# Tile 3's gate and value products as three units of seven half-size products, with the order behind tile 1's middle written anew

## The chip, the cores and the metric

The kernel runs on one core of one Trainium2 chip. The metric is the device time of one execution in microseconds (us), the median over several runs.

## The reference

Two parts, one behind the other. First a linear attention with decay, over blocks of 64 positions (q, k and v are 4 batches × 8 heads × 768 positions × 64):

```python
for b in range(nb):
    intra = np.einsum('bhic,bhjc->bhij', qb, kb) * Dmask[None]
    intra = np.einsum('bhij,bhjd->bhid', intra, vb)
    inter = np.einsum('bhid,bhde->bhie', qb * lam_pow[None], kv_state)
    out[:, :, sl] = intra + inter
    kb_dec = kb * rev_pow[None]
    kv_state = lam_block[None, :, None, None] * kv_state + np.einsum('bhsd,bhse->bhde', kb_dec, vb)
```

Then a gated feed-forward network on the attention's output as x (3072 tokens × 512, inner width 1536):

```python
g = x @ w_gate
silu = g * (1.0 / (1.0 + np.exp(-g)))
val = x @ w_val
return (silu * val @ w_out).astype(np.float32)
```

Inputs and output are float32; the kernel multiplies in bfloat16 and sums in float32.

## The kernel before, in words

**Tiles and groups.** The tokens are cut into 6 FFN tiles of 512 (t = 0 to 5), and the attention into 12 groups of 256 tokens (g = 0 to 11); groups 2t and 2t+1 make tile t's input, `xt`. A state per batch runs from group to group, so the groups of one batch must come in order.

**A group's way through the engines.** SyncE (SP in the profile) loads its k, q and v (`load_fp32`, L103). The keys are cast by `kcast` (L277, mostly ScalarE, ACT), the queries scaled by `qcast` (L281, VectorE, DVE, or GpSimd, POOL), both are turned by one transposing DMA (`dma_transpose`, L265, issued by SP), and v is scaled (`v_scale`, L257). On TensorE (PE) follow `scores` (32 small matmuls; the causal `mask` L356 on DVE carries them to SBUF), `upd_mm` (L390, the state's increments), `inter` (L530, the query with the state) and `intra` (L547, the scores with v). Inter and intra sum into the same two banks; between them ACT reads one column of a bank (`guard`, L523), and intra waits for that. `sadd` (L485, DVE) adds the increments to the state step by step, `kvn` (L503) casts each step for inter, `kvm` (L507) and `kv0c` (L511) pass the state on to the next group of the batch. `evr` (L566) evicts the two banks into `xt`, on ACT with few exceptions.

**An FFN tile.** The inner width is 12 chunks of 128. For tiles 0 to 3, `ffn_gate` (L592) and `ffn_val` (L607) each do 4 matmuls a chunk: 512 columns each, or 256 for half a tile; `HALVED` (L585) names chunks of which each matmul is cut in two. ACT takes the SiLU of the gate (L605), DVE multiplies (L622) into `h`.

Tiles 4 and 5 use a scheme with seven products in place of eight for a 2 × 2 block multiplication. `unit` (L721) takes two chunks of each half of the inner width, so that three units make up a tile; `uprod(t, j, k, i)` (L731) is product k (0 to 6) of unit j, for the gate (i = 0) or the value (i = 1): 4 matmuls of 256 columns, so 14 such products make a unit. Behind k = 0 and k = 1 ACT copies a bank (L759 into the bank Bb, L761 into the buffer es), behind k = 2 and k = 4 DVE adds Bb and es (L763 into the bank E, L765 into es). `silu` (L770) and `mu` (L776) make h out of the four quarters; `mup` (L515) is the quarter whose two inputs both lie in SBUF. The products need sums of the weights (`w_combo`, L686: four for the gate, four for the value; the last, n = 3, overwrites the second-half weights in place) and of x (`x_combo`, L707: four a tile, the last in place). Once the weights are overwritten, no plain chunk from 6 on can be done any more.

The output product is of the same kind for tiles 1 to 5: `hsum` (L665, four sums of h, in pieces along the chunks), `oprod` (L799, product k = 1 to 7 of half a tile, 6 matmuls of 256 columns), `store` (L792). Tile 0 uses plain products (`ffn_out`, L629).

**The order.** Nothing is scheduled by a planner at run time: the calls stand in the order in which each engine gets its instructions, some 800 lines from L838 on. `use(...)` names the banks (of PSUM's eight) that the next helper takes; `unit`, `out_new` and `op_new` take theirs for longer. TensorE runs through its own instructions in that order, and so does every other engine; a wait at the head of an engine's queue holds up all that stands behind it. The DMAs of loads, transposes and stores are issued by SP in their order. Some 1,030 lines in, tile 1's chunks are half done; tile 2's chunks, tile 3's chunks, groups 4 to 11, the output products and the units of tiles 4 and 5 follow, interleaved.

Tile 3 before is 12 gate and 12 value chunks of 512 columns. Groups 8, 9 and 10 are attended between its chunks and behind. Group 10's `inter` (L1422) stands in unit (4, 0) and its `intra` (L1437) in unit (4, 1); group 8's is this, L1302 to L1310:

```python
    use(1, 5); op_new(8)
    inter(8, True)
    use(6, 0); scores(9)
    use(4, 3); upd_mm(9)
    sadd(9, 0)
    guard(8)
    kvn(9, 0, ACTC)
    sadd(9, 1)
    intra(8, False)
```

## Time and profile before

| | us |
|---|---|
| median of 3 runs | 215.95 (215.81 to 216.06) |
| profiled execution, its own time | 215.75 |
| its span | 214.04 |
| TensorE busy | 207.5 |
| VectorE busy | 157.5 |
| ScalarE busy | 131.8 |
| GpSimd busy | 50.9 |

The span is the time between the first and the last instruction in the trace; the execution's own time has 1.71 us around it. An engine's busy time is the union of its instructions (register work, semaphores and the issuing of DMAs are not counted). The chain of waits goes back from the last instruction, at each step to what released it. Times of rows are microseconds from the span's start, and a row such as `117.15 2.59 PE bank L618 x12` gives start, length, engine, output, line and the number of instructions. In the table of groups the numbers behind the bar are busy time, mean nanoseconds of one instruction, and the idle time of the engine ahead of them with what ended it.

### The profile page before, as it was taken

Reading aid. Unit: us, or ns where it says so; the run is one execution under the profiler, and the core shown is the slowest. Engines: PE = TensorE matmul, PEld = TensorE weight load, DVE = VectorE, ACT = ScalarE, POOL = GpSimd, SP = SyncE. Lnnn points to the kernel's source line nnn. Section 1 sums busy time; section 2 is a strip of 40 time slices with the busy share of each in tenths; the row PEclk is TensorE's granted clock in tenths of the full one; section 3 lists DMA queues with packets and bytes.
Section 4 is the critical chain, followed back from the end, with each engine's and each line's share of the span. In section 5 each row is a group of like instructions: output and inputs, shape, how many; then the busy total and the mean of one; then the engine's idle time right before and its main releaser. Section 6 shows DMA issues by size and latency. Waiting matters only on the chain.

```text
span 214.0 us, 6802 instructions
## 1 busy us (share of the span) xinstructions
PE 207.5 (97%) x2801; PEld 153.0 (72%) x2801; DVE 157.5 (74%) x302; ACT 131.8 (62%) x283; POOL 50.9 (24%) x72
## 2 busy tenths in 40 slices
PE   7799999999999999999999999999999999999993
PEld 3466455888886558767654545888888888888883
DVE  1673447679774798889779899999887589982851
ACT  6788576657446443667677385946873677536522
POOL 6585755704472010300101030040200000000200
PEclk9999999999999999999999999999999999999999
DMA  6999999999996697989677869776000500005014
GB/s 187 343 352 373 378 365 324 266 256 222 356 335 132 168 280 188 240 204 261 156 189 163 208 144 248 185 69 228 6 3 3 196 0 3 0 0 199 0 54 147
DMA packets 82177, 39.77 MB, mean 186 GB/s; under 512 B 45410, under 2 KB 77794, under 8 KB 82146
## 3 DMA queue, kind: packets, MB, share of 16 engines
q1 hardware_dynamic: 80946, 38.74, 66.7%
q10 hardware_dynamic: 1200, 0.59, 1.0%
q8 instruction: 22, 0.36, 0.7%
q14 instruction: 9, 0.07, 0.1%
HBM read 28.31 MB, written 6.29 MB: 162 GB/s over the span
## 4 chain that ended last, share of the span: by engine, by line
PE 92%; SPq 3%; DMA 2%; POOL 1%; issue 0%; ACT 0%; DVE 0%
PE bank L814 22%; PE bank L600 20%; PE bank L618 20%; PE bank L755 17%; PE bank L638 5%; SPq L109 2%; DMA v<-in_v_dram 2%; PE bank L541 2%; PE bank L554 2%; PE bank L408 1%; PE bank L347 1%; POOL v_s L260 1%; PE bank L383 1%; PE bank L310 0%; ACT kvf L501 0%
## 5 line engine op out<-in xcount | busy, mean ns | idle before, releaser
L622 DVE TENSOR_TENSOR h<-sil,bank 128x256 bf16<-128x256 bf16 (+1 forms) x67 | 35.0, 532 | 21.4 <-PE bank L618 17.2
L618 PE MATMUL bank<-xt,wv_sb 128*128 128x256 bf16 (+1 forms) x276 | 50.2, 314 | 0.0
L600 PE MATMUL bank<-xt,wg_sb 128*128 128x256 bf16 (+1 forms) x276 | 50.1, 315 | 0.0
L605 ACT ACTIVATE sil<-bank 128x256 bf16<-128x256 f32 (+1 forms) x67 | 31.6, 477 | 22.3 <-PE bank L600 15.7
L618 PEld LDWEIGHTS <-wv_sb 128*128 128x128 bf16 x276 | 26.6, 98 | 14.7
L600 PEld LDWEIGHTS <-wg_sb 128*128 128x128 bf16 x276 | 26.1, 98 | 12.9
L260 POOL TENSOR_TENSOR v_s<-v,dec 128x512 bf16<-128x512 f32 (+1 forms) x15 | 18.6, 1254 | 60.9 <-DMA v<-in_v_dram 19.8
L814 PEld LDWEIGHTS <-h 128*128 128x128 bf16 x240 | 23.5, 98 | 3.6
L814 PE MATMUL bank<-wo_sb,h 128*128 128x256 bf16 x180 | 22.3, 273 | 0.0
L814 PEld LDWEIGHTS <-hs 128*128 128x128 bf16 x180 | 17.5, 98 | 3.4 <-DVE hs L673 0.2
L362 DVE TENSOR_TENSOR ssb<-bank,causal 128x512 bf16<-128x512 f32 x24 | 15.5, 684 | 3.6 <-PE bank L347 3.5
L814 PE MATMUL bank<-wt,hs 128*128 128x256 bf16 x120 | 15.6, 272 | 0.0
L755 PEld LDWEIGHTS <-ws 128*128 128x128 bf16 x144 | 14.0, 98 | 1.8
L755 PE MATMUL bank<-xs,ws 128*128 128x256 bf16 x96 | 13.9, 272 | 0.0
L763 DVE TENSOR_TENSOR bank<-bank,es 128x512 f32<-128x512 f32 x12 | 8.3, 697 | 7.2 <-PE bank L755 4.4
L780 DVE TENSOR_TENSOR h<-sil,bank 128x512 bf16<-128x512 bf16 x18 | 11.8, 679 | 1.5 <-ACT sil L774 1.2
L780 POOL TENSOR_TENSOR h<-sil,es 128x512 bf16<-128x512 bf16 x1 | 1.2, 1162 | 46.7 <-DVE es L765 46.7
L774 ACT ACTIVATE sil<-bank 128x512 bf16<-128x512 f32 x18 | 10.2, 593 | 2.1 <-PE bank L755 2.1
L638 PE MATMUL bank<-wo_sb,h 128*128 128x512 bf16 x48 | 10.9, 379 | 0.0
L755 PE MATMUL bank<-xt,wv_sb 128*128 128x256 bf16 x72 | 10.8, 273 | 0.0
L443 ACT CAST kvn<-kvf 64x256 bf16<-64x256 f32 x22 | 8.9, 403 | 3.1 <-DVE kvf L489 2.7
L278 ACT CAST qk<-kraw 128x1024 bf16<-128x1024 f32 x9 | 9.4, 1042 | 1.8 <-DMA kraw<-in_k_dram 1.8
(127 smaller groups left out, 342.9 us busy)
## 6 DMA issues: line engine op xcount, KB each, us to landing
out_dram<-osb SPq DMA_DIRECT2D x22, 256.0 KB, 2.7
v<-in_v_dram SPq DMA_DIRECT2D x18, 256.0 KB, 4.3
woraw<-in_moe_w_out_dram SPq DMA_DIRECT2D x6, 512.0 KB, 9.1
kraw<-in_k_dram SPq DMA_DIRECT2D x24, 128.0 KB, 3.2
qraw<-in_q_dram SPq DMA_DIRECT2D x24, 128.0 KB, 3.8
wraw<-in_moe_w_gate_dram SPq DMA_DIRECT2D x5, 512.0 KB, 6.9
wraw<-in_moe_w_val_dram SPq DMA_DIRECT2D x5, 512.0 KB, 6.7
kraw<-in_k_dram SPq DMA_DIRECT2D x4, 512.0 KB, 6.3
```

The lines of the kernel that those rows point to most:

```text
L260: eng.tensor_tensor(out=st[("vs", g)][:, h0:h1], in0=st[("v", g)][:, h0:h1].rearrange("p h (s d) -> p h s d", s=2), in1=vfac(g, h0, h1), o ...
L278: fn(out=qk_new(g)[:, 0].rearrange("p s (h d) -> p h s d", h=H), in_=st[("kraw", g)].rearrange("p h (s d) -> p h s d", s=2))
L362: nc.vector.tensor_tensor(out=st[("ssb", g)][:, h2, 2 * c:2 * c + 2].rearrange("p a s n -> p a (s n)"), in0=st[("sp", g, c, h2)].rearrange ...
L600: nc.tensor.matmul(gp[:, n0:n1], wg_sb[:, mc, fs], xt[:, g0:g1, mc].rearrange("p g b n -> p g (b n)"), start=(mc == 0 and n0 == 0), stop=( ...
L605: nc.scalar.activation(sil[:, 0:N], gp[:, 0:N], AF.Silu)
L618: nc.tensor.matmul(vp[:, n0:n1], wv_sb[:, mc, fs], xt[:, g0:g1, mc].rearrange("p g b n -> p g (b n)"), start=(mc == 0 and n0 == 0), stop=( ...
L622: nc.vector.tensor_tensor(out=h_sb[:, fc % FH, b0:b1].rearrange("p b n -> p (b n)"), in0=sil[:, 0:N], in1=vp[:, 0:N], op=ALU.mult)
L638: nc.tensor.matmul(ps, st[("h", t, fc // FH)][:, fc % FH, b], wo_sb[:, fc, c0:c1], start=(fc == 0), stop=(fc == FC - 1))
L755: nc.tensor.matmul(o[i][:, fi * 256:fi * 256 + 256], lhs(c, 2 * j + fi), rhs(c), start=(k < 2 and fi == 0 and c == 0), stop=(c == KH - 1), ...
L774: nc.scalar.activation(sil[half, r], unit_src(t, j, half, r)[0], AF.Silu)
L780: eng.tensor_tensor(out=st[("h", t, half)][:, 2 * j:2 * j + 2][:, :, r:B:2], in0=v3(st[("u", t, j)][4][half, r]), in1=v3(unit_src(t, j, ha ...
L814: nc.tensor.matmul(o, lhs(f), rhs(f), start=(k in (1, 7) and f == 0), stop=(f == FH - 1), skip_group_check=True)
```

## The change

What it does:

- Tile 3 is done in three units of 14 products, like tiles 4 and 5, in place of its 24 chunks. Its sums of x take a buffer of the pool that also holds the transposed queries and keys.
- The sums of the weights come earlier, ahead of tile 3, in 8 calls (they were 10). As they overwrite the second-half weights, tile 2's chunks 6 to 11 now come first (6 to 9 in half tiles), then 0 to 5; `HALVED` names chunks 10 and 11.
- Group 10's inter, guard and intra stand in one place among tile 2's output products. Group 8's stand directly behind each other.
- The order of all that follows tile 1's middle is written anew, with other banks.
- Engines: to POOL go `kcast` of groups 7 and 11, `qcast` of 10 and 11 (`qcast` of 7 was there), `v_scale(7)` and the second half of `v_scale(9)`, `kvm(7)`, `kvn(6, 1)`, `kvn(9, 1)`, all three `kvn` of group 11, `mup` of (3, 1), (4, 0) and (5, 1), and four of tile 5's sums of h. From POOL to DVE go `v_scale(11)`, `kvm(3)` and `kvm(5)`. All evictions from group 3 on are on ACT.

The same before and after: 12 each of scores, updates, inter and intra; the output products; the units of tiles 4 and 5.

```diff
-    HALVED = ((2, 4), (2, 5))
+    HALVED = ((2, 10), (2, 11))
...
-    XS0 = 4
+    XS0 = (3, 4)
...
-            pool, tag = (qkt_pool, "qkt") if t == XS0 else (raw_pool, "raw")
+            pool, tag = (qkt_pool, "qkt") if t in XS0 else (raw_pool, "raw")
```

The part of the new order that holds tile 3 (all lines new in this form):

```diff
+    use(4, 5); op_new(7)
+    oprod(1, 1, 2)
+    oprod(1, 1, 3)
+    oprod(1, 1, 4)
+    inter(7, True)
+    use(0, 3); scores(8)
+    guard(7)
+    intra(7, False)
+    use(6, 7); upd_mm(8)
...
+    v_scale(9, nc.gpsimd, 0, 4)
+    v_scale(9, nc.gpsimd, 4, 8)
...
+    unit(3, 0, (7, 5, 4, 3, 2, 1))
+    uprod(3, 0, 0, 0)
+    hsum(2, 0, 0, 4, 0, 2, nc.vector)
+    x_combo(3, 2, None, nc.vector)
...
     dma_transpose(9)
     load_fp32(10, nc.sync, k, "kraw")
     load_fp32(10, nc.sync, q, "qraw")
+    store(1, 0, 0, 0, 512, None)
+    store(1, 1, 1, 0, 512, None)
+    load_fp32(10, nc.sync, v, "v")
+    silu(3, 0, 0, 1)
+    use(5, 6); upd_mm(9)
     inter(8, True)
+    guard(8)
+    intra(8, False)
+    use(0, 2); scores(9)
     sadd(9, 0)
     kvn(9, 0, ACTC)
     sadd(9, 1)
+    kvn(9, 1, POOLC)
+    sadd(9, 2)
+    mu(3, 0, 1, 0)
+    mask(9, 0, 0)
+    mask(9, 0, 1)
+    hsum(2, 0, 4, 6, 0, 2, nc.vector)
+    evr(8, 0, ACTC)
+    kvn(9, 2, ACTC)
+    unit(3, 1, (6, 0, 5, 2, 3, 7))
+    uprod(3, 1, 0, 0)
+    uprod(3, 1, 1, 0)
+    uprod(3, 0, 4, 1)
+    uprod(3, 1, 0, 1)
+    uprod(3, 1, 2, 0)
+    mup(3, 0, nc.vector)
...
+    kcast(10, ACTC)
+    qcast(10, nc.gpsimd)
     dma_transpose(10)
     load_fp32(11, nc.sync, k, "kraw")
     load_fp32(11, nc.sync, q, "qraw")
     load_fp32(11, nc.sync, v, "v")
+    store(1, 1, 0, 0, 512, None)
+    uprod(3, 1, 4, 0)
+    uprod(3, 0, 6, 1)
+    uprod(3, 1, 5, 0)
+    uprod(3, 1, 3, 1)
+    mu(3, 0, 0, 1)
+    mu(3, 1, 0, 0)
+    hsum(2, 1, 0, 4, 0, 2, nc.vector)
+    uprod(3, 1, 6, 0)
+    uprod(3, 1, 4, 1)
...
+    unit(3, 2, (1, 4, 6, 0, 3, 5))
+    uprod(3, 2, 0, 0)
+    uprod(3, 2, 0, 1)
+    uprod(3, 1, 5, 1)
+    uprod(3, 2, 1, 0)
+    mu(3, 1, 1, 0)
+    hsum(2, 1, 4, 6, 0, 2, nc.vector)
+    uprod(3, 2, 1, 1)
+    uprod(3, 2, 2, 0)
+    uprod(3, 2, 2, 1)
+    uprod(3, 1, 6, 1)
+    uprod(3, 2, 3, 0)
+    silu(3, 2, 0, 0)
+    mu(3, 1, 0, 1)
+    uprod(3, 2, 4, 0)
+    uprod(3, 2, 4, 1)
...
+    mup(3, 1, nc.gpsimd)
+    hsum(2, 2, 4, 6, 0, 2, nc.vector)
+    v_scale(10, nc.gpsimd, 0, 4)
+    kvm(7, nc.gpsimd)
+    v_scale(10, nc.gpsimd, 4, 8)
...
     inter(9, True)
+    use(6, 4); upd_mm(10)
+    use(7, 3); scores(10)
+    guard(9)
+    intra(9, False)
+    kcast(11, POOLC)
+    qcast(11, nc.gpsimd)
```

Tile 2's output products with group 10 in them, and the tail's sums on POOL:

```diff
     oprod(2, 1, 6)
+    x_combo(4, 0, None, nc.vector)
+    oprod(2, 0, 6)
+    x_combo(4, 1, None, nc.vector)
+    hsum(2, 3, 4, 6, 0, 2, nc.vector)
     sadd(10, 0)
     kvn(10, 0, ACTC)
...
+    use(4, 0); op_new(10)
+    oprod(2, 1, 3)
+    inter(10, True)
+    guard(10)
+    oprod(2, 0, 3)
+    use(3, 6); upd_mm(11)
+    intra(10, False)
...
+    hsum(5, 3, 0, 2, 0, 2, nc.gpsimd)
+    mup(5, 1, nc.gpsimd)
+    hsum(5, 0, 2, 4, 0, 2, nc.gpsimd)
+    hsum(5, 2, 2, 4, 0, 2, nc.gpsimd)
+    hsum(5, 3, 2, 4, 0, 2, nc.gpsimd)
+    mup(5, 2, nc.gpsimd)
```

834 lines of the change are left out of this document (395 added, 439 removed).

## The prediction

> **What bounds the kernel now.** I read the page's head first, then the chain of waits, then the busy time by stretch, then the groups by form, and last the timelines around the places that the change touches. A number in the sums has its row quoted ahead of it.
>
> ```profile
> span 214.0 us, 6802 instructions
> PE 207.5 (97%) x2801; PEld 153.0 (72%) x2801; DVE 157.5 (74%) x302; ACT 131.8 (62%) x283; POOL 50.9 (24%) x72
> PE   7799999999999999999999999999999999999993
> PE 92%; SPq 3%; DMA 2%; POOL 1%; issue 0%; ACT 0%; DVE 0%
> ```
> TensorE is busy for 97% of the span and holds 92% of the chain that ended last. Next the chain itself (start, length, engine, work):
>
> ```profile
> 97.01 0.38 PE bank L541 x32
> 98.26 0.97 PE bank L600 x4
> 117.15 2.59 PE bank L618 x12
> 167.86 17.47 PE bank L755 x160
> 210.86 0.28 ACT osb L833
> 211.16 0.29 DVE osb L833
> ```
> From the first tenth of the span to 210.86 each piece begins where the last ended: TensorE is gapless, and it alone sets the end. Here are its unit prices: an FFN matmul of 512 columns takes 2.59/12 = 0.216 us, a half-size product's matmul of 256 columns 17.47/160 = 0.109 us, and the first FFN chunk after an attention block 0.97 instead of 4 × 0.216 = 0.86, so 0.10 for the return. The busy time of the stretch that the change rewrites (columns: stretch; length; PE, PEld, DVE, ACT, POOL busy with counts; granted clock; DMA share; GB/s):
>
> ```profile
> 47.80:110.45 62.65, 62.65 (x975) 45.29 (x976) 50.35 (x93) 35.87 (x79) 14.77 (x13) 1.00 0.94 231
> 110.45:134.47 24.02, 24.02 (x345) 12.23 (x343) 21.58 (x37) 16.29 (x36) 3.10 (x3) 1.00 0.77 189
> 134.47:167.86 33.39, 33.39 (x466) 28.81 (x465) 29.70 (x59) 21.68 (x50) 3.79 (x4) 1.00 0.34 74
> 167.86:210.86 43.00, 42.97 (x393) 38.08 (x390) 29.51 (x59) 24.57 (x52) 1.16 (x1) 1.00 0.16 62
> ```
> The rewritten part starts at 47.80. PE is busy 163.03 of 163.06 us there, at full clock; DVE is next, with 21.58 of 24.02 in the stretch that holds tile 3. So a saving on TensorE is worth its full size as long as the others keep up, and DVE has the least room to.
>
> **The change, part by part.** The prices of what is added on the other engines:
>
> ```profile
> L605 ACT ACTIVATE sil<-bank 128x512 bf16<-128x512 f32 x29 | 17.1, 596 | 11.9 <-PE bank L600 10.5 <-issue 1.2
> L780 DVE TENSOR_TENSOR h<-sil,bank 128x512 bf16<-128x512 bf16 x18 | 11.8, 679 | 1.5 <-ACT sil L774 1.2 <-PE bank L755 0.3
> L763 DVE TENSOR_TENSOR bank<-bank,es 128x512 f32<-128x512 f32 x12 | 8.3, 697 | 7.2 <-PE bank L755 4.4 <-ACT es L761 2.5
> L765 DVE TENSOR_TENSOR es<-bank,es 128x512 f32<-128x512 f32 x12 | 8.2, 685 | 1.0 <-PE bank L755 0.8
> L761 ACT COPY es<-bank 128x512 f32<-128x512 f32 x12 | 6.9, 592 | 1.3 <-PE bank L755 1.2
> L759 ACT COPY bank<-bank 128x512 f32<-128x512 f32 x12 | 6.7, 578 | 0.6 <-ACT sil L774 0.2
> L719 DVE TENSOR_TENSOR xs<-xt,xs 128x512 bf16<-128x512 bf16 x4 | 1.7, 419 | 0.1
> L780 POOL TENSOR_TENSOR h<-sil,es 128x512 bf16<-128x512 bf16 x1 | 1.2, 1162 | 46.7 <-DVE es L765 46.7
> L282 POOL TENSOR_TENSOR qk<-qraw,qdn 128x1024 bf16<-128x1024 f32 x1 | 1.9, 1903 | 11.2 <-DMA qraw<-in_q_dram 11.2
> ```
> *TensorE.* Removed: 24 chunks × 4 matmuls × 0.216 = 20.74. Added: 3 units × 14 products × 4 matmuls × 0.109 = 18.35. That is **−2.4 us**. The other matmuls keep their counts and sizes, and both orders go back from attention to other products 22 times, so these 0.10s cancel. Tile 2's reordered chunks, with other chunks halved, cost nothing: the same number of columns.
>
> *ACT.* Tile 3's 12 activations stay (L605's become L774's). Added are 3 units × 4 copies: 6 × 0.592 + 6 × 0.578 = 7.0; the evictions that DVE did come over and some casts go to POOL. ACT had 98.4 us busy of 163 (the four stretches); with 5 more it is still far from full. Cost nothing as a load; its queue order counts below.
>
> *DVE.* The 12 multiplications stay (0.68 each). Added: 3 × 4 sums, 6 × 0.697 + 6 × 0.685 = 8.3, and four combinations of x, 4 × 0.42 = 1.7. Taken off: two query scalings at 1.22 as POOL gets them, two multiplications, half a value scaling and one whole, a state scaling, four short tail sums, two evictions; put on: the last group's value scaling and two state scalings. Net some 2 us on 131. What the total hides is the place: between the last attention visit of group 7 (106) and the middle of tile 2's output (137) the new order puts 57 DVE instructions (19 of 0.68, 12 of 0.42, 9 of 0.41, 16 of 0.69 to 0.70, one of 1.22), 34.0 us, on 31.2 us of TensorE work. The next fence shows that back to back such an instruction starts 0.60 after the last where it lasts 0.69, so 0.08 overlaps, and the 57 need 34.0 − 4.6 = 29.4. **Fits with 1.8 us to spare**, if nothing lengthens them.
>
> *POOL* gets 17 us more after 47.8: two key casts, two query scalings (1.90), three more multiplications (1.16), state casts, and four of tile 5's sums of 512 columns. For such a sum on POOL no row stands; the bounds are 1.05 to 1.16 (the value scaling and the multiplication of that size, of which I take 1.16), and the sums are issued some 10 us ahead of the products that read them: nothing. It matters for the rows below.
>
> ```profile
> 116.14 0.69 DVE L673 TENSOR_TENSOR hs<-h,hs 128x1024 bf16<-128x1024 bf16 x1
> 116.74 0.95 DVE L680 TENSOR_TENSOR ws<-wg_sb,ws 128x1536 bf16<-128x1536 bf16 x1
> 126.06 2.06 POOL L260 TENSOR_TENSOR v_s<-v,dec 128x512 bf16<-128x512 f32 x2 [10.45 <-DVE qk L282]
> 127.11 1.55 DVE L673 TENSOR_TENSOR h<-h 128x1024 bf16<-128x1024 bf16 x1
> 139.13 2.53 POOL L260 TENSOR_TENSOR v_s<-v,dec 128x512 bf16<-128x512 f32 x2 [11.02 <-PE bank L814]
> 140.75 1.20 DVE L673 TENSOR_TENSOR hs<-h,hs 128x512 bf16<-128x512 bf16 x1
> ```
> A DVE sum of two operands in SBUF takes 0.69 alone. At 127.11 it took 1.55: POOL's scaling was running, ended at 128.12, and the sum ended 0.54 later. At 140.75 a sum of 0.42 took 1.20, until POOL's end at 141.66 and 0.29 more. So a **DVE instruction with both inputs in SBUF that begins inside a POOL instruction finishes only behind it**. The Trainium skill, "SBUF — State Buffer", section "Who interferes with whom", states this as a rule: DVE's second SBUF input comes through a port pair shared with GpSimd, and whoever issues first holds it for the whole instruction. Both pairs of rows agree with it; a reader who took it at its word for every such meeting would arrive at the third rival below.
>
> *The waits that the order makes.* The rows for them:
>
> ```profile
> 77.25 1.63 SPq L268 DMA_TRANSPOSE qkt<-qk  x1
> 87.15 1.90 POOL L282 TENSOR_TENSOR qk<-qraw,qdn 128x1024 bf16<-128x1024 f32 x1 [11.23 <-DMA qraw<-in_q_dram]
> 114.14 1.73 SPq L268 DMA_TRANSPOSE qkt<-qk  x1
> 121.91 0.16 ACT L525 COPY guard<-bank 128x1 f32<-128x1 f32 x1 [0.67 <-PE bank L541]
> 122.87 0.82 ACT L443 CAST kvn<-kvf 64x256 bf16<-64x256 f32 x2 [0.81 <-DVE kvf L489]
> 123.60 1.30 ACT L572 CAST xt<-bank 128x512 bf16<-128x512 f32 x2
> ```
> (1) Group 8's inter, guard and intra now stand next to each other; before, scores and the state update lay between. TensorE waits for the guard copy, 0.16, and two hand-overs that I put at 0.05 each: 0.27. The same in group 10 lies behind an output product and costs nothing. (2) In unit (3,1) the product that needs the copy of A waits on ACT, where guard 0.16, two state casts of 0.82 and an eviction of about 0.65 stand ahead of or among the copies while only some 2.1 us of products are ready: 0.3. (3) Scores of group 5 wait for their transpose 0.1 at most. Other hand-overs (scores of groups 8 and 9, value scaling 9) come out within 0.15 us of just in time, either way; I leave them at 0. Two stores of tile 1, put between group 10's query and value loads on SP, delay v by some 1 us; q lands about 124 and the scaling of v is wanted at 131, so that is hidden.
> (4) Queries land 9.9 us after the transpose ahead of them is issued (87.15 − 77.25). The new order issues group 9's transpose at about 114, as before, so q(10) lands at 124.0 and its scaling holds POOL until 125.9. DVE, without a pause from 117.2 on, comes to the sum hsum(2,1,0,4) at 124.6 and ends it at 126.5 instead of 125.2; mup(3,1) on POOL from about 127.1 catches the next sum the same way, 0.6 more. The sums of unit (3,2)'s k = 2 products, which had some 0.5 in hand (128.1 against 128.6), are then 1.9 − 0.5 = 1.4 late for its k = 4 products. The 0.67 of (1) to (3) hold TensorE up earlier, while DVE is full anyway: they are part of these 1.4 if DVE's queue doesn't move with TensorE, and come on top if it does: 1.4 to 2.1 with both meetings. With the first alone (1.3 − 0.5 = 0.8) it is 0.8 to 1.5. I take 1.3, the first meeting and most of the earlier waits.
> The tail is the same work in the same order, with POOL done ahead: 0.
>
> **Sum.** 215.75 (the profiled execution: 214.04 span and 1.71 around it) − 2.4 + 1.3 = 214.65. That execution lies 0.20 under the median of the runs, so I predict **214.85**. A stall S in general gives 213.55 + S.
>
> **The rivals.** *A: no meeting.* The POOL instructions fall between DVE's sums by luck; q(10) landing 1 us earlier or later suffices. Stall 0 to 0.7: 213.55 to 214.25. For it: TensorE ran 163 us without one gap in the order of before; against it: DVE is the fullest where it starts.
> *B: a second meeting.* q(11) lands about 136 (the transpose behind q(10)'s scaling, 126, plus 9.9), and its 1.9 us on POOL holds up x_combo(4,0), the last sums of tile 2 and so the state sums of group 10 behind them on DVE; inter(10) waits. 0.6 to 1.0 more: S = 1.9 to 2.3, **215.45 to 215.85**, no change.
> *C: slower, DVE becomes the bound between 106 and 137.* Of its 57 instructions 16 have both inputs in SBUF (6 of x, 8 sums of h, one multiplication, one scaling). POOL holds 11.8 us of these 31.2, a share of 0.38. If each meets at that share and loses on average 0.65 us (half of 1.1 plus the restart), DVE needs 29.4 + 16 × 0.38 × 0.65 = 33.4 for 31.2, and the waits at its inputs, 0.7, come on top: S = 3.0, **216.55**. It decides from S above 2.8 (216.38). For it: the two meetings in the old order came from just 3 and 4 POOL instructions in their stretches; against it: they cost TensorE nothing there, and queues shift until instructions no longer meet.
> *D: that the change doesn't do what it says* can't be: the counts come out of the text. Only the clock could differ, and it was 1.00 in all stretches.
>
> **How the numbers follow.** The forecast 0.32 (214.45 to 215.25), A 0.23, B 0.23, C 0.22. Range: A's lowest quarter and C beyond 216.5 are left out, about 0.06 and 0.11, so 213.7 to 216.5. A measurement of this kernel can tell about 0.2% from no change: below 215.52 is faster, above 216.38 slower. Faster: 0.32 + 0.23 + a third of B = 0.63; slower: most of C, 0.19; same 0.18.
>
> **What would show it.** Right in the saving: L755 with 168 matmuls more, L600 and L618 with 48 fewer each, at 0.109 and 0.216, and PE's busy time down by 2.4. Right in the stall: gaps in TensorE's timeline at unit (3,2), ended by DVE sums of line 763, with a sum of line 673 at 1.2 us or more beside a POOL scaling at 124 to 126. A shows TensorE without gaps; B a gap ahead of inter(10) behind L489; C gaps in all three units, and DVE over 95% there. Wrong altogether would be a gap at a transpose's or a load's landing, or at a bank handed over, in the parts that I put at 0.

## The result, and the profile after

The changed kernel takes **218.99 us** (median of 4 runs, 218.29 to 220.12) against 215.95 before: a ratio of 1.0146 (95% interval 1.0103 to 1.0189), so it is slower by 3.0 us. The forecast was 214.85, in a range of 213.7 to 216.5. The profiled execution took 218.98, its span is 217.0. In the table of the experiments below two of the ten runs of e13 and one of the ten of e10 lie more than 1.5% above the fastest of their kernel; the medians count them, the ratios do not.

The head of the page of the changed kernel, and the group that counts its plain gate matmuls:

```profile
span 217.0 us, 6982 instructions
PE 208.5 (96%) x2873; PEld 161.3 (74%) x2873; DVE 163.2 (75%) x306; ACT 135.0 (62%) x290; POOL 67.8 (31%) x87
PE   8899999999999999999999998999999999999994
PE 63%; DMA 12%; DVE 6%; SPq 6%; ACT 5%; issue 3%; POOL 3%; DVEq 0%; ACTq 0%; POOLq 0%
L600 PE MATMUL bank<-xt,wg_sb 128*128 128x256 bf16 (+1 forms) x228 | 38.6, 301 | 0.0
```

228 plain gate matmuls are left of 276, as many as the change removes. TensorE's share of the chain of waits fell from 92% to 63%: the end is now set by several engines in turn. This is how that chain reads in the stretch of tile 3, and at its end (start, length, engine, work):

```profile
126.45 1.49 DVE h L673
...
130.30 0.70 DVE bank L763
...
136.34 4.05 PE bank L814 x36
...
175.84 11.79 PE bank L755 x108
...
208.88 0.40 issue
209.27 0.44 DVE bank L823
209.76 4.10 PE bank L814 x36
213.88 0.28 ACT osb L833
```

The last product now ends at 213.88, before at 210.86: 3.0 later. Half-size products still cost 11.79/108 = 0.109 each. So the saving of 2.4 is in the trace, and it has been given back more than twice. Group 3's update, the last call ahead of the rewritten order, starts at 47.73 instead of 47.35; that 0.4 arose in the start-up, whose order is the same in both (in the traces of the other runs the same call starts between 47.10 and 48.21). The rest, 3.0 + 2.4 − 0.4 = **5.0 us, are products that start late** behind this point.

They are easy to overlook. The busy time by stretch, first of before, then of after (columns: stretch; length; busy time and count of PE, PEld, DVE, ACT, POOL; granted clock; DMA share; GB/s):

```profile
47.35:210.86 163.51, 163.48 (x2217) 124.82 (x2206) 131.50 (x246) 98.42 (x215) 22.97 (x21) 1.00 0.59 149
118.00:147.00 29.00, 29.00 (x449) 19.42 (x447) 26.66 (x47) 19.02 (x43) 4.59 (x4) 1.00 0.81 189
```

```profile
47.73:213.88 166.15, 163.42 (x2290) 132.50 (x2279) 137.09 (x250) 101.63 (x222) 39.95 (x36) 1.00 0.56 149
47.73:118.00 70.27, 69.83 (x1073) 51.27 (x1063) 61.44 (x110) 42.84 (x95) 20.31 (x16) 1.00 0.88 223
118.00:147.00 29.00, 27.08 (x532) 22.78 (x530) 26.73 (x46) 19.91 (x45) 9.17 (x8) 1.00 0.74 181
147.00:213.88 66.88, 66.51 (x689) 58.45 (x687) 48.92 (x96) 38.88 (x83) 10.47 (x12) 1.00 0.15 57
```

TensorE's idle time is 166.15 − 163.42 = 2.73, of which 1.92 lie between 118 and 147, with tile 3 and group 10. But its busy time stayed at 163.4, though 2.4 us of work were taken out: the other 2.3 of lateness count as busy. A matmul of 256 columns is shown 0.27 long while the next can start 0.109 behind it, so the first 0.16 of each wait hides under the matmul ahead, and a wait below 0.16 is not seen as idle at all. To find the lateness I compared the start of each call with the start of the call ahead plus its price.

**Unit (3, 2), 0.9 us.** The timelines of POOL, DVE and PE around it in the changed kernel, and the same meeting later:

```profile
125.74 1.90 POOL L282 TENSOR_TENSOR qk<-qraw,qdn 128x1024 bf16<-128x1024 f32 x1 [5.61 <-PE bank L755]
126.45 1.74 DVE L673 TENSOR_TENSOR h<-h 128x1024 bf16<-128x1024 bf16 x1
128.93 1.17 POOL L780 TENSOR_TENSOR h<-sil,es 128x512 bf16<-128x512 bf16 x1 [1.29 <-DVE es L765]
129.31 1.07 DVE L673 TENSOR_TENSOR h<-h 128x512 bf16<-128x512 bf16 x1
130.30 1.28 DVE L763 TENSOR_TENSOR bank<-bank,es 128x512 f32<-128x512 f32 x2
131.04 1.19 PE L755 MATMUL bank<-xs,ws 128*128 128x256 bf16 x8 [0.55 <-DVE bank L763]
...
138.05 1.90 POOL L282 TENSOR_TENSOR qk<-qraw,qdn 128x1024 bf16<-128x1024 f32 x1 [0.56 <-DMA qraw<-in_q_dram]
138.56 1.94 DVE L673 TENSOR_TENSOR hs<-h,hs 128x1024 bf16<-128x1024 bf16 x1
```

The first sum took 1.74 instead of 0.69 and the second 1.07 instead of 0.42, each beginning inside a POOL instruction and ending behind it. Unit (3, 2)'s products behind the sums of k = 2 came 0.71 and 0.16 late. The meeting with group 11's scaling is there too, 1.94.

**Copies on ACT, 1.1 us,** at output product (1, 1, 6) 0.46, unit (3, 0) 0.31, unit (3, 1) 0.32. **Attention visits, 1.8 us:** from the first of a visit's small matmuls (inter's; for group 8 after, the update's that now stands ahead of it) to the next product, groups 6 to 9 took 1.25, 1.14, 1.17 and 1.27 before; they take 1.56, 1.49, 1.68 and 1.93. **Group 10 and tile 2's output, 0.9 us** in three waits: 0.27 at an output product (143.79), 0.38 in group 10's inter (144.98), 0.22 at unit (4, 0) (147.58). **The tail, 0.45 us.** One of each kind from the timelines of after, the second group being a visit:

```profile
111.55 0.82 ACT L443 CAST kvn<-kvf 64x256 bf16<-64x256 f32 x2
112.28 0.57 ACT L759 COPY bank<-bank 128x512 f32<-128x512 f32 x1
112.90 0.60 PE L755 MATMUL bank<-xs,ws 128*128 128x256 bf16 x4
...
118.32 0.60 ACT L774 ACTIVATE sil<-bank 128x512 bf16<-128x512 f32 x1 [0.33 <-PE bank L755]
119.04 0.16 ACT L525 COPY guard<-bank 128x1 f32<-128x1 f32 x1
119.25 0.45 PE L554 MATMUL bank<-ssb,v_s 64*64 64x64 bf16 x32 [0.34 <-ACT guard L525]
...
135.11 0.44 PE L554 MATMUL bank<-ssb,v_s 64*64 64x64 bf16 x29
136.12 0.22 PE L554 MATMUL bank<-ssb,v_s 64*64 64x64 bf16 x3 [0.57 <-issue]
...
207.14 0.42 DVE L673 TENSOR_TENSOR hs<-h,hs 128x512 bf16<-128x512 bf16 x1
209.27 0.77 DVE L823 TENSOR_TENSOR bank<-bank,osb 128x256 f32<-128x256 f32 x2 [1.71 <-PE bank L814]
209.76 1.47 PE L814 MATMUL bank<-wt,hs 128*128 128x256 bf16 x12 [0.29 <-DVE bank L823]
```

At 112 the product that overwrites the copied bank waits for the copy, and the copy stood behind two state casts in ACT's queue; it is 0.31 late, of which its row could show only 0.15 as idle. At 119 the guard copy stood behind a SiLU. At 136 the last 3 of 32 small matmuls started 0.76 late with nothing to wait for, marked "issue". At 209 DVE began a sum late though its input was ready (the chain above has 0.40 of "issue" there). Together 0.9 + 1.1 + 1.8 + 0.9 + 0.45 = 5.1, which is the 5.0.

### The profile page after: what moved, and what is told of

Same layout as the page of the kernel before. It is cut to its first block, busy times and chain, and to the rows that moved or that the text cites. A ratio compares the mean times of both kernels' runs of the same rounds, so it can differ in the third digit from the quotient of the medians.

```text
span 217.0 us, 6982 instructions
## 1 busy us (share of the span) xinstructions
PE 208.5 (96%) x2873; PEld 161.3 (74%) x2873; DVE 163.2 (75%) x306; ACT 135.0 (62%) x290; POOL 67.8 (31%) x87
## 4 chain that ended last, share of the span: by engine, by line
PE 63%; DMA 12%; DVE 6%; SPq 6%; ACT 5%; issue 3%; POOL 3%; DVEq 0%; ACTq 0%; POOLq 0%
PE bank L755 22%; PE bank L814 16%; PE bank L600 8%; PE bank L618 7%; DMA wraw<-in_moe_w_val_dram 4%; PE bank L638 4%; DMA v<-in_v_dram 3%; SPq L124 3%; DMA qraw<-in_q_dram 3%; DMA kraw<-in_k_dram 2%; PE bank L541 2%; PE bank L554 2%; SPq L116 1%; PE bank L408 1%; SPq L268 1%
## 5 line engine op out<-in xcount | busy, mean ns | idle before, releaser
L622 DVE TENSOR_TENSOR h<-sil,bank 128x256 bf16<-128x256 bf16 (+1 forms) x55 | 26.7, 499 | 18.9 <-PE bank L618 13.4
L600 PE MATMUL bank<-xt,wg_sb 128*128 128x256 bf16 (+1 forms) x228 | 38.6, 301 | 0.0
L618 PE MATMUL bank<-xt,wv_sb 128*128 128x256 bf16 (+1 forms) x228 | 38.3, 301 | 0.0
L605 ACT ACTIVATE sil<-bank 128x256 bf16<-128x256 f32 (+1 forms) x55 | 24.3, 451 | 20.0 <-PE bank L600 13.6
L618 PEld LDWEIGHTS <-wv_sb 128*128 128x128 bf16 x228 | 22.1, 98 | 8.2
L600 PEld LDWEIGHTS <-wg_sb 128*128 128x128 bf16 x228 | 21.5, 98 | 7.9
L755 PEld LDWEIGHTS <-ws 128*128 128x128 bf16 x216 | 20.9, 98 | 4.3 <-issue 1.6
L755 PE MATMUL bank<-xs,ws 128*128 128x256 bf16 x144 | 20.5, 272 | 0.9 <-DVE bank L763 0.5
L780 DVE TENSOR_TENSOR h<-sil,bank 128x512 bf16<-128x512 bf16 x27 | 17.9, 679 | 1.1 <-ACT sil L774 1.1
L755 PE MATMUL bank<-xt,wg_sb 128*128 128x256 bf16 x108 | 15.9, 273 | 0.1
L755 PEld LDWEIGHTS <-wg_sb 128*128 128x128 bf16 x144 | 14.0, 98 | 2.3 <-DVE kvf L489 0.2
L755 PEld LDWEIGHTS <-wv_sb 128*128 128x128 bf16 x144 | 14.0, 98 | 1.9
```

What stands on the lines that cost most here:

```text
L600: nc.tensor.matmul(gp[:, n0:n1], wg_sb[:, mc, fs], xt[:, g0:g1, mc].rearrange("p g b n -> p g (b n)"), start=(mc == 0 and n0 == 0), stop=( ...
L605: nc.scalar.activation(sil[:, 0:N], gp[:, 0:N], AF.Silu)
L618: nc.tensor.matmul(vp[:, n0:n1], wv_sb[:, mc, fs], xt[:, g0:g1, mc].rearrange("p g b n -> p g (b n)"), start=(mc == 0 and n0 == 0), stop=( ...
L622: nc.vector.tensor_tensor(out=h_sb[:, fc % FH, b0:b1].rearrange("p b n -> p (b n)"), in0=sil[:, 0:N], in1=vp[:, 0:N], op=ALU.mult)
L755: nc.tensor.matmul(o[i][:, fi * 256:fi * 256 + 256], lhs(c, 2 * j + fi), rhs(c), start=(k < 2 and fi == 0 and c == 0), stop=(c == KH - 1), ...
L780: eng.tensor_tensor(out=st[("h", t, half)][:, 2 * j:2 * j + 2][:, :, r:B:2], in0=v3(st[("u", t, j)][4][half, r]), in1=v3(unit_src(t, j, ha ...
```

## The experiments

All edits are made to the changed kernel unless it says otherwise. The medians, and the ratio to the kernel before in the same series of runs on the same chip:

| run | median (lowest to highest), us | ratio to before, 95% interval |
|---|---|---|
| changed kernel | 218.99 (218.29 to 220.12) | 1.0146, 1.0103 to 1.0189 |
| e1_sums_early | 218.94 (218.53 to 220.99) | 1.0166, 1.0118 to 1.0215 |
| e2_act_order | 218.34 (217.44 to 219.31) | 1.0120, 1.0086 to 1.0155 |
| e3_update_later | 218.45 (218.22 to 221.44) | 1.0171, 1.0097 to 1.0244 |
| e4_all_moved | 218.60 (217.61 to 219.07) | 1.0126, 1.0094 to 1.0157 |
| e5_mended | 218.90 (218.54 to 219.58) | 1.0134, 1.0107 to 1.0161 |
| e6_pool_back | 218.83 (218.30 to 219.22) | 1.0119, 1.0088 to 1.0150 |
| e7_shift_code | 220.62 (220.43 to 222.86) | 1.0234, 1.0180 to 1.0287 |
| e8_order_again | 218.28 (217.49 to 219.23) | 1.0110, 1.0073 to 1.0147 |
| e9_without_sums | 219.56 (218.45 to 220.64) | 1.0155, 1.0110 to 1.0201 |
| e10_pool_fills | 216.69 (216.23 to 220.05) | 1.0013, 0.9986 to 1.0040 |
| e11_both | 216.61 (216.29 to 217.76) | 1.0005, 0.9972 to 1.0038 |
| e12_old_on_pool | 222.69 (222.22 to 224.32) | 1.0294, 1.0237 to 1.0351 |
| e13_all_known | 217.29 (216.17 to 221.18) | 1.0031, 0.9996 to 1.0065 |
| e14_visits | 218.79 (217.73 to 220.18) | 1.0121, 1.0081 to 1.0160 |

The first four take the waits one kind at a time, then all together.

**e1_sums_early: the two sums of h that met POOL, moved to before the meeting.**

```diff
+    hsum(2, 1, 0, 4, 0, 2, nc.vector)
+    hsum(2, 1, 4, 6, 0, 2, nc.vector)
     uprod(3, 1, 4, 0)
     uprod(3, 0, 6, 1)
...
-    hsum(2, 1, 0, 4, 0, 2, nc.vector)
-    hsum(2, 1, 4, 6, 0, 2, nc.vector)
```

> The changed kernel with one thing moved: the two sums hsum(2,1,0,4) and hsum(2,1,4,6) on VectorE stand ahead of the product uprod(3,1,4,0), before group 10's queries land, instead of behind it; the same work on the same engines. Theory (a POOL instruction that reads SBUF holds up a VectorE instruction with two SBUF inputs until it ends): the two sums fall from 1.74 and 1.07 us to 0.69 and 0.42, TensorE's waits at uprod(3,2,4,0) and (3,2,4,1), 0.87 us together, go, and the time is 217.9 to 218.3 against 219.0. Rival (VectorE is simply full between 106 and 137): the sums cost the same wherever they stand, the lateness is as large at unit (3,2), and the time stays within 0.3 of 219.0.

The time did not change. Timelines of DVE and PE in e1:

```profile
126.90 1.02 DVE L673 TENSOR_TENSOR h<-h 128x1024 bf16<-128x1024 bf16 x2
...
128.57 0.60 PE L755 MATMUL bank<-xt,ws 128*128 128x256 bf16 x4 [0.64 <-DVE es L765]
```

Both sums together take 1.02, unobstructed, and the waits of unit (3, 2) are gone. In their place uprod(3, 1, 6, 0) waits 0.80: the two sums now stand in DVE's queue ahead of the bank sums it needs. The mechanism is right and its worth there is nothing, as DVE has no idle time to move them into. (Its profiled execution, at 220.99 the slowest of its runs, also waited 1.2 and 1.0 for two transposes.)

**e2_act_order: state casts and evictions moved behind the copies of banks on ACT.**

```diff
-    kv0c(5, ACTC)
     kvn(7, 0, ACTC)
     sadd(7, 1)
-    kvn(7, 1, ACTC)
-    evr(6, 1, ACTC)
     oprod(1, 1, 1)
+    kvn(7, 1, ACTC)
...
     uprod(3, 0, 1, 1)
+    kvn(8, 2, ACTC)
+    kv0c(6, ACTC)
...
     uprod(3, 1, 1, 0)
+    evr(8, 0, ACTC)
```

> The changed kernel with ScalarE's queue put in another order at three places, nothing else: the copies behind oprod(1,1,1), uprod(3,0,0,0) and uprod(3,1,0,0) go ahead of state casts and evictions that are wanted later. Theory (each of these three waits of TensorE, 0.46, 0.31 and 0.32 us, is a copy that stands behind work for later): they go, 1.1 us in all, and the time is 217.7 to 218.2. Rival (TensorE is held by VectorE's lateness anyway): the waits go from these places and come back at unit (3,1) or (3,2), so at most 0.4 is won, 218.6 to 219.0.

The three waits of 0.46, 0.31 and 0.32 are gone; inter of group 8 came 0.39 late and uprod(3, 2, 2, 0) 0.41, for the casts that had moved. The median is 0.65 lower, between the theory and its rival, but the intervals of the two ratios overlap: the waits are shown, their worth isn't.

**e3_update_later: group 10's update taken out of the row of attention matmuls.**

```diff
-    use(6, 4); upd_mm(10)
...
     oprod(2, 0, 1)
+    use(6, 4); upd_mm(10)
```

> The changed kernel with upd_mm(10) taken out from between inter(9) and scores(10) and put behind two output products; the same work. In the trace TensorE stands still for 0.76 us in the middle of intra(9), three matmuls before its end, with no semaphore to wait for. Theory (its instructions aren't there yet: a block of 256 is fetched while the one before is used up, and the attention's 240 small instructions use one up in 2 us): with 48 instructions fewer in that burst the standstill goes, 0.6 to 0.8 us, time 218.2 to 218.4. Rival (it is a wait for the guard, the evictions or POOL that the trace names badly): the standstill stays in intra(9) or moves with it, time 218.8 to 219.2.

PE's timeline of e3, where after has 0.76 of standstill:

```profile
134.39 0.45 PE L554 MATMUL bank<-ssb,v_s 64*64 64x64 bf16 x32
134.77 1.48 PE L814 MATMUL bank<-wo_sb,h 128*128 128x256 bf16 x12
```

All 32 matmuls run without a break and the next product starts 0.38 behind their start. The profiled execution took 218.22, 0.76 below that of after; the median, with one run at 221.44, can't carry that difference.

**e4_all_moved: e1, e2 and e3 together,** with a product ahead of group 8's guard, two sums of tile 2 ahead of group 10's masks and `kcast(11)` on ACT.

```diff
     silu(3, 0, 0, 1)
+    uprod(3, 0, 4, 1)
     use(5, 6); upd_mm(9)
...
-    kcast(11, POOLC)
+    kcast(11, ACTC)
```

> All three moves in one kernel, and two more: group 11's key cast goes from POOL to ScalarE and the sums hsum(2,2,0,4) and (2,3,0,4) go ahead of the masks of group 10, away from POOL's query scaling; uprod(3,0,4,1) goes ahead of group 8's attention so that the activation before its guard is done in time. Theory (the 5 us are separate waits, each with its own cause, and they add up): the sum of them is 0.87 + 1.1 + 0.76 + 0.4 for the guard + 0.9 for the waits around group 10 = 4.0, and the time is about 215.0, 214.6 to 215.8, at or below the kernel before. Rival (one full engine stands behind them all): less than half of that, 217.0 or more.

218.60 instead of some 215. The old waits are gone, and three new ones of 0.7 to 0.8 came in: uprod(3, 1, 0, 1) for a mask of group 9, uprod(3, 1, 6, 0) for the bank sums as in e1, oprod(2, 0, 7) for a mask of group 10. So the lateness is not a few misplaced calls: DVE is so tightly packed there (26.73 of 29 us busy between 118 and 147 in after) that a call moved ahead of another makes that one late.

**e5_mended: e4's moves, with the three new waits evaded.**

```diff
-    sadd(9, 2)
     mu(3, 0, 1, 0)
     mask(9, 0, 0)
     mask(9, 0, 1)
+    sadd(9, 2)
...
     v_scale(10, nc.gpsimd, 4, 8)
+    mup(3, 1, nc.gpsimd)
```

> The version of e4 without the waits that its own moves made. Against the changed kernel: ScalarE's order as in e2 but with the third state cast of group 8 ahead of the key cast; hsum(2,1,0,4) and (2,1,4,6) behind mu(3,1,1,0); mup(3,1) behind the value scaling on POOL; both masks of group 10 kept ahead of mu(3,2,0,1); upd_mm(9) between inter(8) and intra(8), with the third state sum of group 9 behind its masks; upd_mm(10) behind two output products as in e3. In e4 three waits of 0.70, 0.80 and 0.78 us, each behind an instruction that I had moved, took the place of those removed. Theory (every hand-over in tiles 2 and 3 is just in time, so each must be placed; no engine is full): these three go, and with the other moves the time is 215.0 to 216.2. Rival (VectorE is full from 106 to 137 whatever the order): waits of the same total come back elsewhere in the units of tile 3, 217.5 to 218.5.

One of the moves cost more than all it mended: uprod(3, 1, 1, 0) came 1.69 late, as it takes a bank that sadd(9, 2) now frees later. And PE's timeline shows a standstill at a place that ran through in after:

```profile
95.50 0.30 PE L554 MATMUL bank<-ssb,v_s 64*64 64x64 bf16 x13
96.79 0.35 PE L554 MATMUL bank<-ssb,v_s 64*64 64x64 bf16 x19 [0.98 <-issue]
```

**e6_pool_back: POOL's added work near tile 3 given back to DVE** (and `kcast(11)` to ACT; the transposes of groups 10 and 11 move with the scalings). It tests whether the meetings are worse than the work they relieve DVE of.

```diff
-    qcast(10, nc.gpsimd)
+    qcast(10, nc.vector)
...
-    mup(3, 1, nc.gpsimd)
+    mup(3, 1, nc.vector)
...
-    kcast(11, POOLC)
-    qcast(11, nc.gpsimd)
+    kcast(11, ACTC)
+    qcast(11, nc.vector)
```

> The changed kernel with what it gave to POOL between 124 and 140 taken back: both query scalings and one multiplication on VectorE (1.22, 1.22 and 0.68 us), group 11's key cast on ScalarE; nothing else moved but the issue of group 10's and 11's transposes with the scalings. Theory (the meetings on the shared way into SBUF cost VectorE as much as POOL takes off it: five sums lasted 1.74, 1.07, 1.39, 1.94 and 0.69 where they take 0.69, 0.42, 0.69, 0.69 and 0.69, so 3.0 to 3.3 us against 3.1 us of work): no change that can be told, 218.5 to 219.4, and every sum of line 673 at its short length. Rival (POOL's help is real): VectorE is 2 to 3 us later at unit (3,2) and group 10, time 220 or more. Other rival (the meetings were the main loss): 217.5 or less.

No difference: 218.83. The sums of h are short again (0.68 three times, 0.41, one 0.88), and DVE pays for it with two scalings of 1.22 and a multiplication of 0.68. What these moves to POOL took from DVE's load they took back in meetings.

**e7_shift_code: 28 more matmuls at the start of the program,** where TensorE waits for the first loads anyway, so that everything behind stands 56 instructions later in TensorE's program.

```diff
-    warm_up(4)
+    warm_up(32, 32)
```

> The changed kernel with 32 warm-up products of 32 columns at the very start in place of 4 of 512, so that all later instructions of TensorE stand 56 places further on in its program; nothing else. Theory (the standstill of 0.76 us in intra(9) is a block of 256 instructions that comes too late because the attention's burst of 240 begins just behind a block's start): the burst now has the border in its middle, the standstill goes, and the time falls by 0.5 to 0.8, to 218.2 to 218.5. Rival (the standstill belongs to that place, whatever the count): it stays at the same three matmuls of intra(9), 218.9 to 219.2.

The standstill left group 9's visit and opened anew in group 4's update; and the later queries met another DVE instruction. From the timelines of PE and DVE in e7:

```profile
52.63 0.32 PE L408 MATMUL bank<-v_s,qk 64*64 64x64 bf16 x15 [0.85 <-issue]
...
140.59 2.02 DVE L719 TENSOR_TENSOR xs<-xt 128x512 bf16<-128x512 bf16 x1
```

The combination of x at 140.59 took 2.02 instead of 0.41 beside POOL's scaling (140.44 to 142.34), and oprod(2, 0, 5) came 1.2 late. These two, 1.20 and the standstill's 1.04 in place of 0.76, make 1.5 of the 1.6 by which e7 is slower than the changed kernel: both by where an event falls, not by added work.

**e8_order_again: the moves of e2 and e3 without the two that hurt; e9_without_sums: the same without the moves of DVE's and POOL's calls.** In e8, beside these, the sums stand behind a multiplication instead of ahead of the products:

```diff
     mu(3, 1, 1, 0)
+    hsum(2, 1, 0, 4, 0, 2, nc.vector)
     hsum(2, 1, 4, 6, 0, 2, nc.vector)
...
-    mup(3, 1, nc.gpsimd)
...
     v_scale(10, nc.gpsimd, 4, 8)
+    mup(3, 1, nc.gpsimd)
```

> A second try at a version without the waits. Against the changed kernel: ScalarE's order as in e5, with the third state cast of group 9 moved behind the copies of unit (3,2) too; the sums of tile 2 and POOL's multiplication as in e5; group 9's update and group 8's guard left as in the changed kernel (e5's shift there held a bank back and cost 1.69 us); upd_mm(10) behind two output products, and upd_mm(7) behind an output product and a gate chunk, so that neither the burst of group 9 nor that of group 6 uses up a block of code while the next is fetched. Theory (separate waits, no full engine): what is left of the 5.0 us is the guard of group 8 (0.4), some 0.2 to 0.4 in unit (3,2), 0.2 at unit (4,0): lateness of 1.0 to 1.4 against 2.4 saved, so 214.6 to 215.4, below the kernel before. Rival (VectorE is full, so what is taken away returns within tile 3): 217.0 or more, with one wait of over 0.7 us for VectorE in units (3,0) to (3,2).

> The kernel of e8 without its two moves on VectorE and POOL: the sums hsum(2,1,*), (2,2,0,4) and (2,3,0,4), mup(3,1) and group 11's key cast stand where the changed kernel has them, so that they meet POOL's scalings again; ScalarE's order and the two updates as in e8. Theory (the meetings are worth what they cost in the changed kernel, 0.87 at unit (3,2) and 0.9 around group 10, less the part that ScalarE's order gave back): 0.9 to 1.7 above e8, with sums of line 673 over 1 us beside POOL instructions. Rival (they are worth nothing once the copies are in time): within 0.3 of e8.

e8 is 1.3 below e9 by the medians, inside the 0.9 to 1.7 of the theory, and 1.0 by the ratios, whose intervals overlap. In e9 uprod(3, 2, 4, 0) and (3, 2, 4, 1) come 0.99 late again, which fits the theory; but its trace also waits 1.23 and 0.64 at 90 and 104 us, where the order of the two is the same, so the run does not price the forecast's meeting. e8 is only 0.7 below the changed kernel: the units run through, and seven waits of 0.17 to 0.55 stand between 133 and 147 us, at tile 2's output products, group 10 and unit (4, 0). Three of them the changed kernel has too; four are new, where x_combo(4, 0) took 1.13 and a sum of h 1.14 beside POOL.

**e10_pool_fills and e11_both: POOL's instructions without their reads,** in the changed kernel and in e8. POOL's casts and scalings of groups 7, 10 and 11 and its multiplication in tile 3 are left out; POOL fills their tiles with a constant.

```diff
     def qcast(g, eng=nc.vector):
+        if eng is nc.gpsimd and g in FILL:
+            eng.memset(qk_new(g)[:, 1], 0.5)
+            return
...
+    FILL = (7, 10, 11)
```

> The changed kernel in which POOL fills its tiles with a constant in place of reading and scaling: the key casts of groups 7 and 11, the query scalings of 7, 10 and 11, the value scalings of 7 and 10, the state scaling of 7 and the multiplication mup(3,1) are left out, everything else is as in the changed kernel. POOL writes the same tiles but reads nothing from SBUF, so no VectorE instruction can meet it; VectorE has neither more nor less to do. Theory (meetings make the lateness of VectorE, which costs TensorE 0.87 us in unit (3,2) and 0.9 around group 10 in the profiled run): these waits go, 1.5 to 1.9 us, time 217.0 to 217.6, and every sum of line 673 between 118 and 140 has its short length. Rival (VectorE is full there without any meeting): at most 0.5 us is won, 218.5 or more. What stays in either case is ScalarE's order (1.1), the guard (0.4) and the fetch of code (1.1).

> The kernel of e8 with the same things left out as in e10. e8 has ScalarE's copies in time and two updates moved out of the bursts. Theory (meetings, ScalarE's order and the fetch of code are what the change lost, and they add): of the 5.0 us there remain the guard of group 8 and its neighbour (0.8) and some 0.5 of small ones, so the saving of 2.4 shows at last: 214.6 to 215.6, below the kernel before. Rival (the order is short of slack everywhere, so that the next waits take their place): 216.5 to 218.

DVE's timeline of e10 (its line 690 is line 673 of the others):

```profile
127.53 0.69 DVE L690 TENSOR_TENSOR h<-h 128x1024 bf16<-128x1024 bf16 x1
...
138.06 0.68 DVE L690 TENSOR_TENSOR hs<-h,hs 128x1024 bf16<-128x1024 bf16 x1
```

The sums that took 1.74 and 1.94 take 0.69 and 0.68, the waits of unit (3, 2) and at group 10 are gone, and the median is 2.3 below that of the changed kernel (2.9 by the ratios, 1.0013 against 1.0146). That bounds what hangs on the work left out from above: the fills also start without the landings of k, q and v, so transposes are issued earlier. What it leaves is as telling: without the meetings between 118 and 140 the kernel is level with the one before, not 2.4 faster, and its trace still has the ACT waits of 0.45, 0.31 and 0.33, the guard's 0.47 and 0.76 of standstill in group 9. (Its profiled execution, 218.11, is slower than its median for another reason: it waits 1.22 for a transpose at 95.90.) e11 takes both away and comes no further (expected were 214.6 to 215.6): 2.9 of lateness against before are left, in guard (8) 0.49, inter (8) 0.39, and smaller ones. Three of those, 0.2 to 0.4 each at 67 to 78 us, aren't the change's: e12's trace, of the old order on the same chip, has them too.

**e12_old_on_pool: the kernel before, with the two query scalings on POOL.**

```diff
-    qcast(10, nc.vector)
+    qcast(10, nc.gpsimd)
...
-    qcast(11, nc.vector)
+    qcast(11, nc.gpsimd)
```

> The kernel before with the query scalings of groups 10 and 11 on POOL in place of VectorE, nothing else. Theory (the old order has slack on VectorE, 2 to 3 us idle in 110 to 135, so meetings there cost TensorE nothing): 215.7 to 216.3, with at least one sum of line 673 lengthened beside POOL. Rival (a meeting costs TensorE its length wherever it happens): 217 or more.

It took 6.4 us more, not half a microsecond. Timelines of POOL and SP (SPq is its queue) and TensorE's waits in e12, then SP's timeline before:

```profile
126.14 2.56 POOL L260 TENSOR_TENSOR v_s<-v,dec 128x512 bf16<-128x512 f32 x2 [10.26 <-DMA v<-in_v_dram]
128.67 1.90 POOL L282 TENSOR_TENSOR qk<-qraw,qdn 128x1024 bf16<-128x1024 f32 x1
130.59 1.68 SPq L268 DMA_TRANSPOSE qkt<-qk  x1
148.97 1.59 SPq L268 DMA_TRANSPOSE qkt<-qk  x1
...
PE bank L383 <- DMA qkt<-qk: 4.3, 2, 2.6
```

```profile
126.04 1.69 SPq L268 DMA_TRANSPOSE qkt<-qk  x1
139.88 3.45 SPq L268 DMA_TRANSPOSE qkt<-qk  x1
```

On POOL the scaling stood behind the scaling of v, which waited for its load; the transposes were issued 4.6 and 9.1 later, and the scores of groups 10 and 11 started 2.8 and 1.8 late. One meeting is in it: from 146 to 149.5 us a DVE sum of weights and the second scaling held each other up (2.39 instead of 0.68, 2.64 instead of 1.90), and a product came 1.02 late. The run was meant to price the meeting in the old order; most of what it prices is a queue.

**e13_all_known: e8 with everything learned,** and **e14_visits: the changed kernel with only groups 7's and 8's visits nearer to their old form,** scores and update between inter and intra (for group 8 the update alone).

```diff
     inter(7, True)
-    use(0, 3); scores(8)
     guard(7)
+    use(0, 3); scores(8)
+    use(6, 7); upd_mm(8)
     intra(7, False)
-    use(6, 7); upd_mm(8)
...
-    use(5, 6); upd_mm(9)
     inter(8, True)
     guard(8)
+    use(5, 6); upd_mm(9)
     intra(8, False)
```

e13 alone also has group 10's masks ahead of two sums of tile 2 again, where e8 had moved them back, and puts tile 4's first sums of x behind group 10's state sums:

```diff
-    x_combo(4, 0, None, nc.vector)
-    x_combo(4, 1, None, nc.vector)
...
+    x_combo(4, 0, None, nc.vector)
+    x_combo(4, 1, None, nc.vector)
     x_combo(4, 3, None, nc.vector)
```

> All that is known put together, without leaving out work. Against e8: the masks of group 10 stand ahead of the sums hsum(2,2,0,4) and (2,3,0,4) again, as oprod(2,0,1) waited 0.55 us for them; x_combo(4,0) and (4,1) stand behind the state sums of group 10, as POOL's query scaling had drawn the first out from 0.42 to 1.13 us; group 7 has scores(8) and upd_mm(8), group 8 has upd_mm(9) between inter and intra. Theory (separate waits that add): 0.55 + 0.6 around group 10 + 0.3 + 0.3 for the two visits less than e8, so 216.3 to 216.8, and still not below the kernel before, because POOL's scalings go on meeting VectorE. Rival (waits come back): 217.5 or more.

> The changed kernel with two attention visits in the old form: group 7 as inter, scores(8), upd_mm(8), intra with the guard's copy behind the first two, and group 8 as inter, upd_mm(9), intra, scores(9). Nothing else is moved. Theory (in the changed kernel intra stands right behind the guard, and TensorE waits out ScalarE's copy): the visits take 1.2 and 1.4 us from inter to the next product in place of 1.49 and 1.68, and the time falls by 0.3 to 0.6, to 218.3 to 218.7. Rival (the visit's length is set by what comes after, the banks and the copies): no change of over 0.2, 218.8 to 219.2.

e13 is 1.7 below the changed kernel by the medians, 2.5 by the ratios, and level with the one before (1.0031, 0.9996 to 1.0065): by placing calls, without leaving out work, about half of the lateness goes. In its best run, 216.17, only waits of 0.2 to 0.4 are left. e14's median is 0.2 lower, within the spread, and the visits did not get shorter as the theory had it: in its trace those of groups 7 and 8 take 1.54 and 1.75 (1.49 and 1.68 in after), as a transpose, 0.27, and a bank, 0.36, held them up instead; the copy for uprod(3, 0, 2, 0) came 0.53 late instead of 0.31. No version here beats the kernel before.

## Why the prediction was wrong

*The saving* was right to a tenth: the counts and the prices of 0.109 and 0.216 held, and the busy time did not fall only since lateness counts as busy.

*Steps (2) and (4) and the second meeting* were right in place, and near in size. The copy of A in unit (3, 1) was put at 0.3 and cost 0.32. q(10)'s scaling began at 125.74 (foreseen 124.0), held the sum of h until 128.19, and mup(3, 1) caught the next one; the stall behind the two was 0.87, which is what one meeting had been put at (0.8; both 1.4). Rival B's meeting with group 11's scaling came on top of the forecast's, as B had it; the waits around group 10 are 0.9, in B's 0.6 to 1.0. So B's mechanism is in the trace, but B's S of 1.9 to 2.3 is still less than half of what was lost. POOL's four sums in the tail took 1.15 to 1.16 each and cost nothing, as said.

*The step that failed* is the last sentence of (1) to (3): "Other hand-overs (scores of groups 8 and 9, value scaling 9) come out within 0.15 us of just in time, either way; I leave them at 0." The sum S was 1.3 for a lateness of 5.0. What stood there in place of 0:

- copies on ACT behind casts at two more places, 0.46 and 0.31. Step (2) worked out one such place; the others have the same shape.
- the visits. (1) put group 8's at 0.27 and the others at nothing; all four of groups 6 to 9 became longer, 1.8 in all. 0.47 of it is group 8's guard, which stood behind a SiLU on ACT, a queue that (1) left out, and 0.76 is the standstill in group 9's, of which no row before gave a hint.
- 0.45 in the tail, put at 0 since the order there is the same. It stands in the traces of after, e1, e2, e3, e7 and e9 and not in those of the other versions, e14 among them, whose tail is the same.

Outside these steps lie 0.4 in the start-up.

*"Fits with 1.8 us to spare"* for DVE was right as arithmetic and wrong as comfort. Between 118 and 147 DVE was busy for 26.73 of 29 us, hardly more than before (26.66). But tile 3's plain chunks needed DVE only to hand their banks back, and a unit needs two sums of DVE in each bank before it can go on: in experiments e1, e4 and e5 calls moved forward there made others late. **Rival C** gave the right side, from S above 2.8, by another way: e10 gives all that hangs on the POOL work it leaves out at most 2.9, which includes the forecast's meeting, and leaves the rest. The sentence "a gap ... at a bank handed over, in the parts that I put at 0" named what would make the prediction wrong, and that is what happened.

The range ended at 216.5 since its costs were bounded only where a mechanism had been named. Hand-overs known to be just in time "either way" can only add: an early one gains nothing, as TensorE has no gap to give back.

What stays open: the tail's 0.45 and the start-up's 0.4 were not separated by a run, and the sum of parts is that of one execution; the medians move with the landings of the loads.

## What to carry to other kernels

Work taken from the engine that sets the end brings every other engine's result due earlier by as much, so price the slack of each hand-over first, and where many come out just in time add a share of the lateness for each instead of zero for all. A busy time that does not fall although work was removed is the sign of such lateness: compare starts with starts plus prices, not idle times. A call moved to another engine also moves everything that its new queue makes late (e12: two calls, 6.4 us), and relieves DVE of nothing where it then meets DVE's own instructions.

## What the runs showed of the hardware

**TensorE can stand still in a train of small matmuls with nothing to wait for.** The standstills marked "issue" of this kind lie in trains of equal matmuls without a semaphore between them. In group 9's visit it is 0.76 in after, 0.63 in e1, 0.46 in e2, 0.20 in e6, 0.76 in e10 and 0.27 in e14, which all keep group 10's update there, and none in the versions that took it out (e3, e4, e5, e8, e9, e11, e13). In group 6's visit it is 1.17 in e5 (0.98 of it idle) and 0.33 in e6; in or behind group 4's update 1.04 in e7 and 0.40 in e6 and e9. Counted in instructions of TensorE that had started (matmuls and weight loads), they stand after 4025 to 4029 of them, 2747 to 2749, and 1467 to 1469: some 1280 apart, 5 times 256. The row of the profile's page for the DMA queue that fetches the program, in after:

```profile
q8 instruction: 22, 0.36, 0.7%
```

22 packets of 16 KB for 2 × 2873 instructions are 261 each. Group 9's visit has 120 small matmuls, with their weights 240 instructions, in 1.2 to 1.9 us; half-size products need 13 us for as many (120 × 0.109). In after the packet ahead of the standstill ran from 133.41 to 134.71, and the instructions went on at 136.12, 1.41 behind it. In the others at these places they went on 1.3 to 1.5 behind the end of a packet, and in none of the 16 traces does the first instruction behind such a border start less than 1.2 behind its packet. e3 took 48 instructions out of that visit, so that the border was reached later, and the standstill went; e7 shifted the program by 56 and it went elsewhere. That the fetch is the cause is argued from these numbers; no run changed the fetch itself. The Trainium skill, "Runtime: NRT & Kernel Launch", section "Instruction fetch mechanics", says that the program is refilled in blocks of 256 instructions and that the cost of crossing one is mostly hidden. The block's size agrees with the 261 per packet; in a train of short matmuls the cost was not hidden.

A second kind marked "issue" is not explained: three waits of 0.2 to 0.4 at 67 to 79 us, at tile 0's output products, in the traces of e5 to e7 and e10 to e14 and in none of the others. They keep to their matmuls when e7 shifts the program, and e12 has them in the old order. So medians of different series are best compared by their ratios to before.

**When POOL and DVE meet, the one that begins second waits.** In the meetings of tiles 2 and 3 shown above that is DVE. At 87 us of the changed kernel it is POOL: its query scaling took 2.25 instead of 1.90 beside a DVE sum of weights that had begun earlier; in e9 that sum began inside the scaling and took 2.47 instead of 0.95, and a product came 1.23 late (in e5 2.58, and 0.94 late).

**Whether an order without slack widens the spread is open.** In series of 4 to 7 runs the kernel before spread over 0.25 to 1.0 us, the changed kernel and its versions over 0.9 to 3.2 in 4 to 6. But longer series of the kernel before spread over 1.4 (15 runs), 2.1 (11) and 3.0 (19), and the eight runs of e13 that its ratio counts over 3.1. When a transpose lands is one source of it (e1 and e10).
